# Folding the first batch's gate weights on GpSimd and ScalarE, with a fourth query buffer and a new order of TensorE's steps

## The chip, the cores and the metric

The kernel runs on one core of one Trainium2 chip. The metric is the device time of one execution in microseconds (us); the median of the runs shown stands for the kernel. A core has five engines, each of which takes its instructions in order: TensorE (PE in the profile), VectorE (DVE), ScalarE (ACT), GpSimd (POOL) and SyncE (SP), which here issues nearly all DMA transfers.

## The reference

Four batches, 12800 rows of 128 channels, 49 agents. An attention in two steps through the agents is followed by a gated convolution:

```python
a2k = sm(agents, k)              # softmax over the 12800 keys
agent_v = a2k @ v                # 49 x 128 per batch
q2a = sm(q, agents)              # softmax over the 49 agents
x = q2a @ agent_v

gate_pre = sum(conv_w[t] * shift(x, t) for t in range(5))
gate = 1 / (1 + exp(-gate_pre))
out = (gate * (x @ w_val)) @ w_out
```

All of it is float32.

## The kernel before

A batch's rows are cut into ten **units** of 1280 rows, and for the last part into 25 **chunks** of 512. Units are counted through the batches too: u10 is batch 1's first; chunks likewise, g25 is batch 1's first. The steps of the program have short names, and the list `order` gives the order in which TensorE takes them:

- `k b.u`: scores of a unit of keys (L375), 16 matmuls. ACT copies them out of PSUM (L401), DVE takes maxima (L410).
- `m b` (two steps): the maximum over all keys of a batch, as a bias for the exponentials.
- `v b.u`: exponentials on ACT (L470), a transpose of 32x32 blocks on DVE (L385), and matmuls that add up the agents' values in the bank `av` (L479).
- `f b` (five steps, `fold_weights`): agent values, convolution and weights are folded into small stationary matrices, so that the convolution runs on the agents' 49 weights and not on 128 channels. The first step normalises the agent values (`avT`, L534), multiplies them by the taps on POOL (`gw`, L539) and finds a scale (`rs`). The second does the value matmul (L562) and builds `wst`: a float16 high part and what it leaves over, for the gate (`gate_weights` L605 and `gate_rest`, through L580) and for the value (`val_weights`, L586 to L602), with copies on ACT (L620, L624). The third transposes `wst` in eight matmuls (L634) into `stat`, which DVE (L645) and ACT (L649) copy, and scales the output weight on POOL (L659). The fourth (L670) and fifth (L696) do the output weight.
- `q b.u`: scores of a unit of queries, then the softmax over agents: block transpose and row maximum on DVE (L385, L720), subtraction on POOL (L725), exponential on ACT (L733), sums and weights on DVE (L738 to L747, buffer `qw`), and a split of the weights into float16 parts in the buffer `pt`: L754 on ACT, L759 and L769 on POOL.
- `t b.u`: transposes a unit's `pt` into rows of `x`. For the first four units TensorE does it (L824), with copies by ACT (L831) and DVE (L836); for all others a DMA transpose that SP issues (L810). Then SP issues two copies of rows of x, shifted by a row for each tap, into the tile `x2` (L859), from unit 4 on once for a pair of units. POOL copies a few columns ahead of a new pair (L794).
- `g t`, `a t`, `o t`: gate (five matmuls L897 and one with the shifted rows L901), value (L924, L928) and output (L967 to L969) of a chunk. Between them stand ACT's tanh `th` (L910), DVE's product `h` (L937), its split on ACT (`hh`, L943) and POOL (`hl`, L948); ACT writes the result `ob` (L981) and SP sends it (L996).

Every step adds its operations to a planner (`Plan`), with a cost in microseconds for each and the names of the buffers that it reads and writes. TensorE keeps the order of the list. On every other engine, and for the DMAs on SP, the planner simulates its costs and takes among what is ready the operation with the longest tail of work behind it; the order that comes out is the program's. Loads of k, q and v go through a ring of eleven buffers (L368) and are issued as buffers come free.

`qw` and `pt` are rings of three, used by the unit's number:

```python
qw = ring(3, [P, NBLK, A], F32, "qw")
pts = ring(3, [P, NBLK, P], F16, "pt")
```

PSUM has two banks `sc` that all score steps and the transposes on TensorE use in turn, so a score step waits until the bank of the step before the last has been read.

Of the kernel before, what the change touches and what calls it, by code (L numbers as in the profile page):

```python
# [9 lines left out]
F32 = mybir.dt.float32  # L10
F16 = mybir.dt.float16
# [6 lines left out]
P = 128  # L18
# [5 lines left out]
NBLK = 10  # L24
# [13 lines left out]

NLOAD = 11
NT_, NH = 3, 3  # L40
NX = 4
CUT = 2
NOB = 4
# [23 lines left out]
class Plan:  # L67
# [11 lines left out]
    def add(self, engine, us, fn, reads=(), writes=(), moved=0.0, key=None, urge=0.0):  # L79
        i = len(self.steps)  # L80
        need = set()
        for x in reads:
            need |= self.wrote.get(x, set())
        for x in writes:
            need |= self.wrote.get(x, set()) | self.read.get(x, set())
        for x in reads:
            self.read.setdefault(x, set()).add(i)
        for x in writes:
            self.wrote[x], self.read[x] = {i}, set()
        self.steps.append((engine, us, fn, need, moved, key))  # L90
        self.urge.append(urge)
# [84 lines left out]
def tile_agent_attention_gated_conv(  # L176
# [25 lines left out]
    def ring(n, shape, dtype, name, pool=const):  # L202
        return [pool.tile(shape, dtype, name=f"{name}{i}") for i in range(n)]
# [9 lines left out]
    ets = ring(3, [P, NBLK, AP_], F32, "eT")  # L213
    sts = ring(2, [P, NBLK, AP_], F32, "sT")
    qmx = ring(2, [P, NBLK], F32, "qmx")
    qw = ring(3, [P, NBLK, A], F32, "qw")
    qsm = ring(2, [P, NBLK], F32, "qsm")
    qr = ring(2, [P, NBLK], F32, "qr")
    pts = ring(3, [P, NBLK, P], F16, "pt")
    x1s = ring(NX, [P, PAD + SEG], F16, "x1_")  # L220
    x2s = ring(3, [P, SEG], F16, "x2")
    ths = ring(NT_, [P, CH], F32, "th")
# [280 lines left out]
    avT = const.tile([P, A], F32, name="avT")  # L503
    mx = const.tile([P, 2], F32, name="mx")
    gw = const.tile([P, TAPS, A], F32, name="gw")
    rs = const.tile([P, 2], F32, name="rs")
    wo = const.tile([P, C], F32, name="wo")
    ro = const.tile([P, 1], F32, name="ro")
# [2 lines left out]
    def fold_weights(b):  # L511
# [92 lines left out]
        def gate_weights():  # L604
            dve.tensor_scalar_mul(ghi, gw, rs[:, 0:1])  # L605

        def gate_rest():
            gw3, hi3 = threes(gw), threes(ghi)
            twos = wst[:, 0:TAPS, 2 * A :].rearrange("p k (i r) -> p k i r", r=2)
            for r in range(2):  # L610
                rest(twos[:, :, :, r], gw3[:, :, :, r], 0, hi3[:, :, :, r])
            rest(x2g[:, :, 0:THREES], gw3[:, :, :, 2], 0, hi3[:, :, :, 2])
            rest(x2g[:, :, THREES:], gw[:, :, 3 * THREES :], 0, ghi[:, :, 3 * THREES :])

        w_ = ("wst", x)
        add("dve", 0.4, gate_weights, ["gw", "rsg"], [(*w_, "g")])
        add("dve", 1.2, val_weights, [at_v], [(*w_, "v"), "mxv"])
        add(
            "act", 0.4,
# [4 lines left out]
            "act", 0.22, lambda: nc.scalar.copy(out=wst[:, TAPS, A : 2 * A], in_=vhi),  # L624
            [(*w_, "v")], [(*w_, "e")],
        )
        add("dve", 0.7, gate_rest, ["gw", (*w_, "g")], [(*w_, "r")])
        yield
        pw_, at_w = small(b)
        pw = pw_.bitcast(F16)[:, 0 : (TAPS + 3) * P]  # L630
# [77 lines left out]
    def queries(b, u):  # L708
        g = b * NU + u
        x = g % 2  # L710
        i = slot_of["q", b, u]
        ps, at = bank()
        sT, d, e, w, r, sm = sts[x], qw[g % 3], qw[g % 3], qw[g % 3], qr[x], qsm[x]
        pt = pts[g % 3]
        sa = sT[:, :, 0:A]
        add("pe", 1.07, lambda: score_matmuls(b, ld[i], ps), [("ld", i), ("ld2", i)], [at], key="sc")
        add("dve", 0.84, lambda: transpose_blocks(sT, ps[:, :, 0:GT]), [at], [("sT", x)])
        add(
            "dve", 0.62,
            lambda: nc.vector.tensor_reduce(out=qmx[x], in_=sa, axis=AX.X, op=ALU.max),  # L720
            [("sT", x)], [("qmx", x)],
        )
        add(
            "pool", 1.05,
            lambda: nc.gpsimd.tensor_tensor(  # L725
                out=d, in0=sa, in1=qmx[x].unsqueeze(2).to_broadcast([P, NBLK, A]),
                op=ALU.subtract,
            ),
            [("sT", x), ("qmx", x)], [("qw", g % 3)],
        )  # L730
        add(
            "act", 0.6,
            lambda: nc.scalar.activation(out=e, in_=d, func=AF.Exp, scale=SCALE),  # L733
            [("qw", g % 3)], [("qw", g % 3)],
        )

        def sums():
            nc.vector.tensor_reduce(out=sm, in_=e, axis=AX.X, op=ALU.add)  # L738
            nc.vector.scalar_tensor_tensor(
                out=sm, in0=sm, scalar=1.0 / QS, in1=tiny, op0=ALU.mult, op1=ALU.add  # L740
            )
            nc.vector.reciprocal(out=r, in_=sm)

        add("dve", 0.95, sums, [("qw", g % 3)], [("qr", x)])
        add(
            "dve", 0.68,
            lambda: nc.vector.tensor_tensor(  # L747
                out=w, in0=e, in1=r.unsqueeze(2).to_broadcast([P, NBLK, A]), op=ALU.mult
            ),
            [("qw", g % 3), ("qr", x)], [("qw", g % 3)],  # L750
        )
        p_ = ("pt", g % 3)
        add(
            "act", 0.58, lambda: nc.scalar.copy(out=pt[:, :, A : 2 * A], in_=w),  # L754
            [("qw", g % 3)], [(*p_, 0)],
        )
        add(
            "pool", 0.44,
            lambda: nc.gpsimd.tensor_scalar(  # L759
                out=pt[:, :, 2 * A :].rearrange("p n (i r) -> p n i r", r=2),  # L760
                in0=w[:, :, 0 : 3 * THREES].rearrange("p n (i r) -> p n i r", r=3)[:, :, :, 0:2],
                scalar1=1.0, scalar2=0.0,
                op0=ALU.mult, op1=ALU.add,
            ),
            [("qw", g % 3)], [(*p_, 2)],
        )
        add(
            "pool", 1.09,
            lambda: nc.gpsimd.tensor_tensor(  # L769
                out=pt[:, :, 0:A], in0=w, in1=pt[:, :, A : 2 * A], op=ALU.subtract  # L770
            ),
            [("qw", g % 3), (*p_, 0)], [(*p_, 1)],
        )
    def on_pe(b, u):
        g = b * NU + u
# [25 lines left out]

    def transposes(b, u):
        g = b * NU + u
        pt = pts[g % 3]
        p_ = ("pt", g % 3)
        if not on_pe(b, u):
            dst = unit_rows(g)
            add(
# [17 lines left out]
                    identity=ident16,  # L826
                )

        add("pe", 0.65, matmuls, [("pt", g % 3, n) for n in range(3)], [at], key="t")
        add(  # L830
            "act", 0.65, lambda: nc.scalar.copy(out=dst[:, 0], in_=ps[:, 0, 0 : HB * P]),  # L831
            [at], [("x1", g // 2 % NX, g % 2)],
# [220 lines left out]
    for t in range(len(chunks) + 2):  # L1053
# [8 lines left out]
    kinds = {"m": "max", "f": "fold"}  # L1062
    order = (
# [25 lines left out]
    )  # L1089
    first = [(kinds.get(x[0], x[0]), *map(int, x[1:].split("."))) for x in order.split()]  # L1090
    for w in first:
# [70 lines left out]
```

## Time and profile before

| | |
|---|---|
| three runs | 432.86, 429.33, 430.62 us |
| median | 430.62 us |
| profiled execution | 431.12 us, its span 429.1 us |
| granted TensorE clock, mean | 0.988 |
| busy PE, DVE, ACT, POOL | 403.5, 296.1, 300.5, 226.5 us |
| DMA moved | 127.62 MB |

The span runs from the first to the last instruction. A row of the timeline has start, duration, engine, line, operation, output<-inputs and, in brackets, how long the engine had been idle and what ended that. Durations of matmuls contain a pipeline's depth, so that of back-to-back matmuls the starts are read, not the durations. A row of the windows has busy us (and instructions) of PE, PEld (weight loads), DVE, ACT and POOL, then the granted clock, the DMA engines' busy share and GB/s.

### The profile page before, as it was taken

What the parts mean: (1) busy time and instruction counts of PE and PEld (TensorE: products, weight loads), DVE (VectorE), ACT (ScalarE), POOL (GpSimd) and SP (SyncE); (2) the same over time, 40 slices, a digit from 0 to 9 for tenths busy, and PEclk for the clock granted to TensorE, in tenths of its full rate; (3) what the DMA queues carried; (4) which work ended last, traced back from release to release, by engine and by line L of the source; (5) the groups of instructions that cost most, each with busy time, mean ns of one, the idle gap of its engine ahead of it and who ended that gap; (6) DMA issues with size and microseconds to landing.
All of it is one profiled execution on the core that took longest, in us unless ns stands there. A gap on an engine that the chain in (4) does not pass through costs nothing.

```text
span 429.1 us, 10055 instructions
## 1 busy us (share of the span) xinstructions
PE 403.5 (94%) x3907; PEld 196.1 (46%) x3907; DVE 296.1 (69%) x567; ACT 300.5 (70%) x520; POOL 226.5 (53%) x258
## 2 busy tenths in 40 slices
PE   4879899999989999999999899999998899999995
PEld 2367244346545443445555343345554444434442
DVE  4666889867866978666785876667685588566231
ACT  2474468788856677778866576778984377787875
POOL 1002347664756565555467372764475466777543
PEclk9989899999999999999999999999999899999999
DMA  8999999999999999999999999999999987454833
GB/s 321 420 415 413 374 368 367 280 292 290 409 299 258 341 302 310 339 297 346 276 410 317 333 295 269 287 329 295 332 400 292 313 200 195 133 158 158 206 133 122
DMA packets 75129, 127.62 MB, mean 297 GB/s; under 512 B 50466, under 2 KB 50850, under 8 KB 75084
## 3 DMA queue, kind: packets, MB, share of 16 engines
q1 hardware_dynamic: 74940, 126.87, 95.4%
q8 instruction: 30, 0.49, 0.5%
q10 hardware_dynamic: 144, 0.13, 0.2%
q14 instruction: 15, 0.12, 0.1%
HBM read 79.25 MB, written 26.21 MB: 246 GB/s over the span
## 4 chain that ended last, share of the span: by engine, by line
PE 70%; DMA 18%; DVE 5%; issue 3%; ACT 1%; POOL 1%; SPq 1%; DVEq 0%; ACTq 0%; POOLq 0%
PE gate L897 21%; PE sc L375 16%; DMA x<-pt 8%; PE av L479 6%; PE val L924 4%; PE gate L901 4%; PE out L967 4%; DMA ld<-kT 4%; PE val L928 4%; PE out L969 4%; PE out L968 4%; DMA x<-x 3%; DMA ld<-vP 3%; POOL hl L948 1%; DVE wst L580 1%
## 5 line engine op out<-in xcount | busy, mean ns | idle before, releaser
L948 POOL TENSOR_TENSOR hl<-h,hh 128x512 f16<-128x512 f32 (+1 forms) x101 | 116.7, 1157 | 88.6 <-ACT hh L943 88.1
L897 PE MATMUL gate<-x,stat 128*128 128x512 f16 (+1 forms) x500 | 124.3, 378 | 1.6 <-ACT th L910 1.6
L937 DVE SCALAR_TENSOR_TENSOR h<-th,val 128x512 f32<-128x512 f32 x100 | 67.7, 677 | 71.1 <-PE out L968 35.7
L375 PE MATMUL sc<-ld,ag_sb 128*32 128x320 f32 x1280 | 102.1, 447 | 7.5 <-DMA ld<-kT 7.5
L910 ACT ACTIVATE th<-gate,unscale 128x512 f32<-128x512 f32 x100 | 68.3, 683 | 30.4 <-PE gate L901 28.4
L981 ACT ACTIVATE ob<-out,oscale 128x512 f32<-128x512 f32 x98 | 67.2, 686 | 19.8 <-PE out L969 18.7
L897 PEld LDWEIGHTS <-stat 128*128 128x128 f16 x505 | 45.8, 97 | 65.4 <-issue 16.6
L943 ACT CAST hh<-h 128x512 f16<-128x512 f32 (+1 forms) x101 | 61.5, 609 | 11.0 <-DVE h L937 10.5
L725 POOL TENSOR_TENSOR qw<-sT,qmx 128x490 f32<-128x490 f32 x40 | 41.5, 1039 | 44.1 <-DVE qmx L720 44.0
L375 PEld LDWEIGHTS sc<-ld,ag_sb 128*32 128x32 f32 x1280 | 36.3, 111 | 59.0 <-issue 27.6
L479 PE MATMUL av<-ld,eT 128*32 128x129 f32 (+1 forms) x1400 | 49.6, 276 | 1.5 <-DVE eT L385 1.2
L479 PEld LDWEIGHTS av<-ld,eT 128*32 128x32 f32 (+1 forms) x1400 | 46.1, 115 | 7.7 <-DVE eT L385 2.0
L401 ACT COPY ks<-sc 128x640 f32<-128x640 f32 x40 | 27.7, 692 | 28.0 <-PE sc L375 26.1
L769 POOL TENSOR_TENSOR pt<-qw,pt 128x490 f16<-128x490 f32 x40 | 45.2, 1132 | 2.5 <-ACT pt L754 2.0
L470 ACT ACTIVATE e<-ks,kbias 128x320 f32<-128x320 f32 x80 | 39.4, 553 | 4.4 <-DVE eT L385 2.9
L901 PE MATMUL gate<-x,stat 95*128 95x512 f16 x100 | 38.2, 382 | 3.2 <-DMA x<-x 3.2
L385 DVE STREAM_TRANSPOSE sT<-sc 128x640 f32<-128x640 f32 x40 | 33.5, 837 | 10.4 <-PE sc L375 10.1
L385 DVE STREAM_TRANSPOSE eT<-e 128x640 f32<-128x640 f32 x40 | 33.2, 835 | 10.4 <-ACT e L470 7.2
L967 PE MATMUL out<-hh,wo 128*128 128x512 f16 x98 | 37.5, 382 | 1.8 <-ACT ob L981 1.8
L410 DVE TENSOR_REDUCE kmx<-ks 128x2 f32<-128x640 f32 x39 | 31.5, 812 | 11.0 <-ACT ks L401 11.0
L924 PE MATMUL val<-x,stat 128*128 128x512 f16 x100 | 38.2, 382 | 0.3 <-DVE h L937 0.3
L928 PE MATMUL val<-x,stat 95*128 95x512 f16 x100 | 38.1, 381 | 0.0
(127 smaller groups left out, 397.7 us busy)
## 6 DMA issues: line engine op xcount, KB each, us to landing
ld<-kT SPq DMA_DIRECT2D x40, 640.0 KB
ld<-qT SPq DMA_DIRECT2D x40, 640.0 KB
ld<-vP SPq DMA_DIRECT2D x39, 645.0 KB
outT<-ob SPq DMA_DIRECT2D x48, 512.0 KB
x<-x SPq DMA_DIRECT2D x18, 375.0 KB
x<-x SPq DMA_DIRECT2D x18, 100.0 KB
outT<-ob SPq DMA_DIRECT2D x3, 256.0 KB
x<-x SPq DMA_DIRECT2D x4, 187.5 KB
```

Of the source, the lines that this page charges most:

```text
L375: nc.tensor.matmul(out=out[g * BLK : (g + 1) * BLK, j, 0:GT], lhsT=ag_sb[:, b, j * BLK : (j + 1) * BLK], rhs=src[:, g * GT : (g + 1) * GT] ...
L385: nc.vector.transpose(out=out.rearrange("p n (j i) -> p j n i", j=2), in_=in_.rearrange("p j (n i) -> p j n i", i=BLK),)
L479: nc.tensor.matmul(out=av[o + j : o + j + cols, 0 : C + 1], lhsT=et[:, n, j : j + cols], rhs=vt[:, n, :], start=(u == 0 and n < 2), stop=( ...
L897: nc.tensor.matmul(out=pg, lhsT=stat[:, k, :], rhs=x1[:, c : c + w], start=(k == 0), stop=False,)
L901: nc.tensor.matmul(out=pg, lhsT=stat[0 : TAPS * X2R, TAPS + 1, :], rhs=x2[0 : TAPS * X2R, o2 : o2 + w], start=False, stop=True,)
L910: lambda: nc.scalar.activation(out=th, in_=pg, func=AF.Tanh, scale=unscale[:, 0:1]),
L924: nc.tensor.matmul(out=pv, lhsT=stat[:, TAPS, :], rhs=x1s[(b * NCH + n0 // CH) // 5 % NX][:, PAD + o2 : PAD + o2 + w], start=True, stop=False,
L928: nc.tensor.matmul(out=pv, lhsT=stat[0 : TAPS * X2R, TAPS + 2, :], rhs=x2[0 : TAPS * X2R, o2 : o2 + w], start=False, stop=True,)
L937: lambda: nc.vector.scalar_tensor_tensor(out=h, in0=th, scalar=1.0, in1=pv, op0=ALU.add, op1=ALU.mult),
L943: "act", 0.16 + 0.42 * scale, lambda: nc.scalar.copy(out=hh, in_=h),
L948: lambda: nc.gpsimd.tensor_tensor(out=hl, in0=h, in1=hh, op=ALU.subtract),
L981: lambda: nc.scalar.activation(out=ob[:, o : o + w], in_=po, func=AF.Copy, scale=oscale),
```

## The change

In the first batch the gate weights leave DVE. POOL scales them into a new float32 tile `gs`, ACT rounds that into the float16 high part, and POOL subtracts in four instructions what is left over. DVE keeps the value weights. The other batches stay as they were. The rings `qw` and `pt` get four buffers. The list for TensorE is written anew: many steps change places with their neighbours. The diff, with the first, a middle and the later lines of the list:

```diff
+NPT = 4
-    qw = ring(3, [P, NBLK, A], F32, "qw")
+    qw = ring(NPT, [P, NBLK, A], F32, "qw")
-    pts = ring(3, [P, NBLK, P], F16, "pt")
+    pts = ring(NPT, [P, NBLK, P], F16, "pt")
+    gs = const.tile([P, TAPS, A], F32, name="gs")
...
+        def gate_scaled():
+            nc.gpsimd.tensor_scalar(
+                out=gs, in0=gw, scalar1=rs[:, 0:1], scalar2=1.0, op0=ALU.mult, op1=ALU.mult
+            )
+
+        def gate_rest_pool():
+            def less(out, full, hi):
+                nc.gpsimd.tensor_tensor(out=out, in0=full, in1=hi, op=ALU.subtract)
+
+            gs3, hi3 = threes(gs), threes(ghi)
+            twos = wst[:, 0:TAPS, 2 * A :].rearrange("p k (i r) -> p k i r", r=2)
+            for r in range(2):
+                less(twos[:, :, :, r], gs3[:, :, :, r], hi3[:, :, :, r])
+            less(x2g[:, :, 0:THREES], gs3[:, :, :, 2], hi3[:, :, :, 2])
+            less(x2g[:, :, THREES:], gs[:, :, 3 * THREES :], ghi[:, :, 3 * THREES :])
...
-        add("dve", 0.4, gate_weights, ["gw", "rsg"], [(*w_, "g")])
+        if b == 0:
+            add("pool", 0.4, gate_scaled, ["gw", "rsg"], ["gs"])
+            add("act", 0.4, lambda: nc.scalar.copy(out=ghi, in_=gs), ["gs"], [(*w_, "g")])
+            add("pool", 1.0, gate_rest_pool, ["gs", (*w_, "g")], [(*w_, "r")])
+        else:
+            add("dve", 0.4, gate_weights, ["gw", "rsg"], [(*w_, "g")])
...
-        add("dve", 0.7, gate_rest, ["gw", (*w_, "g")], [(*w_, "r")])
+        if b:
+            add("dve", 0.7, gate_rest, ["gw", (*w_, "g")], [(*w_, "r")])
...
     (in queries and transposes: g % 3 becomes g % NPT for qw and pt)
...
-        "v0.5 v0.6 v0.7 v0.8 v0.9 f0 t0.0 q0.1 f0 f0 k1.0 f0 k1.1 q0.2 g0 k1.2 f0 t0.1 a0 q0.3 "
-        "k1.3 q0.4 k1.4 g1 t0.2 q0.5 a1 g2 k1.5 o0 a2 t0.3 t0.4 g3 a3 o1 q0.6 g4 o2 a4 t0.5 "
+        "v0.5 v0.6 v0.7 v0.8 v0.9 f0 t0.0 f0 q0.1 k1.0 f0 k1.1 f0 q0.2 g0 k1.2 f0 t0.1 a0 q0.3 "
+        "k1.3 k1.4 q0.4 g1 t0.2 q0.5 a1 g2 k1.5 o0 a2 t0.3 t0.4 g3 a3 o1 q0.6 g4 o2 a4 t0.5 "
...
-        "v2.6 v2.7 g42 a42 o40 t2.1 g43 a43 o41 g44 a44 o42 t2.2 q2.3 v2.8 v2.9 g45 a45 o43 f2 "
-        "q2.4 f2 k3.0 g46 a46 o44 k3.1 g47 a47 o45 t2.3 f2 g48 a48 o46 f2 g49 a49 o47 f2 t2.4 "
+        "v2.6 v2.7 g42 a42 o40 t2.1 g43 a43 o41 g44 o42 a44 t2.2 q2.3 v2.8 v2.9 o43 g45 a45 f2 "
+        "g46 a46 o44 f2 q2.4 k3.0 g47 a47 o45 g48 f2 t2.3 k3.1 a48 o46 f2 g49 a49 o47 t2.4 "
...
-        "g66 o64 a66 q3.2 v3.6 v3.7 g67 a67 o65 t3.1 g68 a68 o66 g69 a69 o67 t3.2 q3.3 v3.8 "
-        "v3.9 g70 a70 o68 f3 g71 a71 o69 f3 q3.4 g72 o70 a72 f3 t3.3 g73 a73 f3 o71 g74 f3 "
+        "g66 a66 o64 q3.2 v3.6 v3.7 g67 a67 o65 t3.1 g68 a68 o66 g69 v3.8 v3.9 a69 g70 t3.2 "
+        "o67 q3.3 a70 o68 f3 g71 a71 o69 f3 q3.4 g72 o70 a72 t3.3 g73 a73 f3 o71 g74 f3 a74 "
...
```

More of the change, by code (lines that the diff above doesn't have):

```diff
@@ L712, in queries @@
         ps, at = bank()
-        sT, d, e, w, r, sm = sts[x], qw[g % 3], qw[g % 3], qw[g % 3], qr[x], qsm[x]
-        pt = pts[g % 3]
+        sT, d, e, w, r, sm = sts[x], qw[g % NPT], qw[g % NPT], qw[g % NPT], qr[x], qsm[x]
+        pt = pts[g % NPT]
         sa = sT[:, :, 0:A]
@@ L728, in queries @@
             ),
-            [("sT", x), ("qmx", x)], [("qw", g % 3)],
+            [("sT", x), ("qmx", x)], [("qw", g % NPT)],
         )
@@ L733, in queries @@
             lambda: nc.scalar.activation(out=e, in_=d, func=AF.Exp, scale=SCALE),
-            [("qw", g % 3)], [("qw", g % 3)],
+            [("qw", g % NPT)], [("qw", g % NPT)],
         )
@@ L742, in sums @@
             nc.vector.reciprocal(out=r, in_=sm)
-        add("dve", 0.95, sums, [("qw", g % 3)], [("qr", x)])
+        add("dve", 0.95, sums, [("qw", g % NPT)], [("qr", x)])
         add(
@@ L749, in queries @@
             ),
-            [("qw", g % 3), ("qr", x)], [("qw", g % 3)],
+            [("qw", g % NPT), ("qr", x)], [("qw", g % NPT)],
         )
-        p_ = ("pt", g % 3)
+        p_ = ("pt", g % NPT)
         add(
             "act", 0.58, lambda: nc.scalar.copy(out=pt[:, :, A : 2 * A], in_=w),
-            [("qw", g % 3)], [(*p_, 0)],
+            [("qw", g % NPT)], [(*p_, 0)],
         )
@@ L764, in queries @@
             ),
-            [("qw", g % 3)], [(*p_, 2)],
+            [("qw", g % NPT)], [(*p_, 2)],
         )
@@ L771, in queries @@
             ),
-            [("qw", g % 3), (*p_, 0)], [(*p_, 1)],
+            [("qw", g % NPT), (*p_, 0)], [(*p_, 1)],
         )
@@ L803, in transposes @@
         g = b * NU + u
-        pt = pts[g % 3]
-        p_ = ("pt", g % 3)
+        pt = pts[g % NPT]
+        p_ = ("pt", g % NPT)
         if not on_pe(b, u):
@@ L827, in matmuls @@
                 )
-        add("pe", 0.65, matmuls, [("pt", g % 3, n) for n in range(3)], [at], key="t")
+        add("pe", 0.65, matmuls, [("pt", g % NPT, n) for n in range(3)], [at], key="t")
         add(
```

34 rows, old and new, of the table order are left out of this document.

## The prediction

> **What bounds the kernel now.** I read the page's parts 1 and 2 first, then who waited for whom, then the timeline around each place where TensorE (PE) waits.
>
> ```profile
> PE 403.5 (94%) x3907; PEld 196.1 (46%) x3907; DVE 296.1 (69%) x567; ACT 300.5 (70%) x520; POOL 226.5 (53%) x258
> ```
>
> PE is busy 403.5 of the span's 429.1 us. Who it waited for (us in total, times, longest):
>
> ```profile
> PE sc L375 <- DMA ld<-kT: 7.5, 7, 5.8
> PE gate L901 <- DMA x<-x: 3.2, 2, 2.0
> ```
>
> The 7.5 us are for the first keys, before anything that the change touches. What else is longer than a microsecond lies, along the timeline, in four places: the fold of the first batch (L634), two waits for shifted rows x<-x (L901), and two where ScalarE (ACT) came late; their rows stand below. The rest I regard as bound by PE's own work, which the change leaves equal: the same matmuls in another order.
>
> The fold, in order of time:
>
> ```profile
> 41.20 1.28 PE L375 MATMUL sc<-ld,ag_sb 128*32 128x320 f32 x16
> ...
> 41.49 0.21 DVE L534 TENSOR_TENSOR avT<-out,den 128x49 f32<-128x49 f32 x1
> ...
> 41.78 0.60 POOL L539 TENSOR_TENSOR gw<-avT,moe_sb 128x245 f32<-128x245 f32 x1 [2.16 <-DVE avT L534]
> ...
> 42.41 0.42 PE L562 MATMUL val<-avT,moe_sb 128*128 128x49 f32 x2
> ...
> 42.50 0.47 DVE L605 TENSOR_SCALAR wst<-gw,rs 128x245 f16<-128x245 f32 x1
> ...
> 42.88 0.48 DVE L836 COPY x<-sc 128x640 f16<-128x640 f16 x1
> 43.01 0.40 ACT L620 COPY wst<-wst 128x245 f16<-128x245 f16 x1 [1.01 <-DVE wst L605]
> ...
> 43.28 0.94 DVE L580 SCALAR_TENSOR_TENSOR wst<-gw,rs,wst 128x75 f16<-128x75 f32 x4
> ...
> 43.96 0.44 PE L634 MATMUL gate<-ident,wst 128*128 128x128 f16 x5 [1.12 <-DVE wst L580]
> ...
> 44.09 0.20 DVE L586 TENSOR_REDUCE mx<-val 128x1 f32<-128x49 f32 x1
> ...
> 45.02 0.53 DVE L580 SCALAR_TENSOR_TENSOR wst<-val,rs,wst 128x30 f16<-128x30 f32 x3
> ...
> 45.42 0.42 PE L634 MATMUL gate<-ident,wst 128*128 128x128 f16 x3 [1.02 <-DVE wst L580]
> ...
> 45.46 0.84 DVE L385 STREAM_TRANSPOSE sT<-sc 128x640 f32<-128x640 f32 x1
> ...
> 45.77 1.79 PE L375 MATMUL sc<-ld,ag_sb 128*32 128x320 f32 x16
> ...
> 47.90 3.28 PE L375 MATMUL sc<-ld,ag_sb 128*32 128x320 f32 x32
> ...
> 51.11 1.25 PE L897 MATMUL gate<-x,stat 128*128 128x512 f16 x5
> ...
> 51.90 1.09 POOL L769 TENSOR_TENSOR pt<-qw,pt 128x490 f16<-128x490 f32 x1 [0.19 <-ACT pt L754]
> ...
> 53.85 0.72 PE L824 MATMUL sc<-ident,pt 128*128 128x128 f16 x10
> ```
>
> VectorE (DVE) does gate weights, gate rests and value weights one behind the other, and PE waits 1.12 and 1.02 us for them. A pass of 16 score matmuls takes 1.21 us from its start to the next (41.20 to 42.41), but the one at 45.77 takes 1.72 to the L670 transpose that follows, and two passes from 47.90 take 3.21 instead of 2.42. In 40 to 50 us the granted clock is 0.83:
>
> ```profile
> 40.00:50.00 10.00, 7.80 (x77) 3.75 (x81) 8.01 (x29) 3.11 (x6) 1.99 (x3) 0.83 1.01 366
> ...
> 60.00:70.00 10.00, 10.00 (x85) 4.52 (x82) 9.35 (x19) 8.59 (x15) 8.14 (x10) 1.00 1.02 344
> ```
>
> So the fold costs more than its waits: the slower matmuls add 0.51 + 0.79 us.
>
> **The change part by part.**
>
> *The first fold.* Off DVE come L605, 0.47, and four rests, 0.94: 1.41 us. The new chain begins at about 42.4, where gw stands (L539 ends at 42.38): a GpSimd (POOL) scaling of 245 elements, an ACT cast, four POOL subtractions (three of 75 elements, one of 20). Nothing like them stands here, but their neighbours do:
>
> ```profile
> L759 POOL TENSOR_SCALAR pt<-qw 128x300 f16<-128x300 f32 x40 | 17.9, 447 | 28.5 <-DVE qw L747 21.4 <-DMA x<-pt 7.0
> ```
>
> For the scaling I take 0.45, the row nearest in size (it could be 0.60 as L539). A POOL TENSOR_TENSOR takes 0.60 for 245 elements and 1.09 for 490, so 2.0 ns an element and 0.11 fixed: 0.26 for 75, 0.15 for 20, 0.93 for the four. The cast costs 0.40 as L620, and delays ACT's own copy L620 to 43.7, which is still early. With 0.05 at each of three hand-overs the chain ends near 42.4 + 0.45 + 0.40 + 0.93 + 0.15 = 44.3. Meanwhile DVE does the x copy and the value weights, which took 1.46 us (44.09 to 45.55), from 42.43: done at 43.9, or 44.4 with the x copy (L836, 0.48) first.
>
> PE's order there is new too: the value matmul L562 stands ahead of q0.1, so PE waits from 41.20 to 41.75 for avT (ready 41.70), then 0.42, q0.1 1.21, k1.0 1.21: 44.6, and the eight transposes find all weights ready. Both old waits, 2.14 us, become one of 0.5. PE then needs q0.1's bank, whose DVE transpose (0.84) starts at 44.4 rather than 45.46, so k1.1 runs 45.3 to 46.5, then L670 and q0.2, and g0 starts near 47.9: 3.2 us earlier. But the next step that needs a chain is t0.1. It stood 2.74 us behind g0 (51.11 to 53.85), and its operand ended 7.53 us after q0.1's DVE transpose began (45.46 to 52.99). That gives 44.4 + 7.53 = 51.9 instead of 53.85: 1.9 us. And DVE is busy 9.35 of 10 us at 60 to 70, so what lasts is about DVE's own 1.41. I take **1.5 us**, between -0.5 (POOL at half that pace, as L747 below shows for DVE: weights 1.4 us later, near 45.7, past the old 45.42) and 3.2.
>
> By the Trainium skill (SBUF — State Buffer, section "SBUF: two separate sides") a VectorE instruction with two SBUF inputs and a GpSimd instruction lock each other out for their whole length. By that, each meeting of a moved POOL instruction with such a DVE instruction would cost up to 0.85 us, and one of them on the path would leave 0.7 of the 1.5. The trace bears the rule out where such pairs meet:
>
> ```profile
> 211.28 1.15 POOL L948 TENSOR_TENSOR hl<-h,hh 128x512 f16<-128x512 f32 x1 [1.23 <-ACT hh L943]
> ...
> 211.45 1.51 DVE L747 TENSOR_TENSOR qw<-qw,qr 128x490 f32<-128x490 f32 x1
> ...
> 345.07 0.65 DVE L747 TENSOR_TENSOR qw<-qw,qr 128x490 f32<-128x490 f32 x1
> ```
>
> L747 takes 0.65 alone and 1.51 beside L948. In the first fold DVE's work reads one operand from PSUM, so I charge nothing.
>
> *Four buffers.* With three, unit u's write of pt waits until unit u-3's DMA transpose has read it. That stops ACT, which runs in order, twice:
>
> ```profile
> 127.39 0.60 ACT L754 CAST pt<-qw 128x490 f16<-128x490 f32 x1 [3.72 <-DMA x<-pt]
> ...
> 128.63 1.24 PE L897 MATMUL gate<-x,stat 128*128 128x512 f16 x5 [1.36 <-ACT th L910]
> ...
> 328.50 0.60 ACT L754 CAST pt<-qw 128x490 f16<-128x490 f32 x1 [2.63 <-DMA x<-pt]
> ...
> 329.74 0.38 PE L967 MATMUL out<-hh,wo 128*128 128x512 f16 x1 [1.83 <-ACT ob L981]
> ```
>
> Queued behind the blocked cast are th and ob, for which PE waits. With four, the write waits for u-4, whose transpose SP, also in order, issued one earlier. So 1.36 and 1.83 us go. The first counts whole: **1.36**. What is late next after the second is shown here:
>
> ```profile
> 237.13 0.39 PE L901 MATMUL gate<-x,stat 95*128 95x512 f16 x1 [1.19 <-DMA x<-x]
> ...
> 311.51 0.59 ACT L754 CAST pt<-qw 128x490 f16<-128x490 f32 x1
> ...
> 315.15 8.08 SPq L810 DMA_TRANSPOSE x<-pt  x1
> ...
> 324.43 4.06 SPq L810 DMA_TRANSPOSE x<-pt  x1
> ...
> 332.61 1.66 SPq L859 DMA_DIRECT2D x<-x  x2
> ...
> 340.01 0.59 PE L901 MATMUL gate<-x,stat 95*128 95x512 f16 x1 [2.02 <-DMA x<-x]
> 340.39 0.63 PE L924 MATMUL val<-x,stat 128*128 128x512 f16 x1
> ...
> 342.52 0.53 PE L520 MATMUL av<-fold,av 128*128 128x64 f32 x2
> ```
>
> L520 is the first f3, so the L901 before it belongs to g70, and the one at 237.13, likewise ahead of f2, to g45. Both chunks begin at a batch's unit 8 and need the shifted copy of units 8 and 9. For g70 these are u28 and u29 (counted through the batches): ACT's cast of u28 runs at 311.51, SyncE (SP) stands 8.08 us with its transpose, u29's follows at 324.43, the shifted copy at 332.61, and PE waits for it until 340.01. There the matmuls also take 0.63 rather than 0.38 us for a while. If that copy doesn't come earlier, PE only waits longer here, and the 1.83 is given back; if it comes earlier by as much, all stays. I count half: **0.92**, ends 0 and 1.83.
>
> *The order.* Mostly steps change places by one or two, with equal sums. Two moves touch the waits for x<-x. Ahead of g45 (237.13) now stands o43, three matmuls of 0.22, 0.65 us of work under the 1.19 wait: **0.65** gained. Ahead of g70 no longer stand q3.3 (1.21) and o67 (0.65): 1.86 us of cover gone, so PE comes to the same wait earlier and does that work later. If the copy stays where it is, the loss is 1.86; if it comes that much earlier, nothing. Half: **0.93** lost. The other moves I set at nothing, hidden by PE's continuous work; they could add or take one wait of the size seen, 1 to 2 us either way.
>
> Sum: 1.5 + 1.36 + 0.92 + 0.65 - 0.93 = 3.5 us. The profiled execution took 431.12, 2.0 more than its span and 0.5 above the median of 430.62 (429.33 to 432.86). 431.12 - 3.5 - 0.5 gives **427.1**, 0.8% faster than the median.
>
> **The rivals.**
>
> *The shifted copies come in time* (chance 0.27). Transposes freed from the third buffer are issued earlier, and g45 and g70 find their rows. Then 1.36 + 1.83 + 1.19 + 2.02 go, and the slow matmuls behind g70 (eight of about 0.2 extra, 1.7); with the fold 9.6 us: 421.0, or 422.2 if the copy at g45 stays late. For it: four buffers are on that path. Against: the row of u28's cast names no wait for a buffer; ACT did it late in its own order, and SP stood 8.08 us with one issue.
>
> *DMA sets the pace* (0.15). DMA's busy share is over 1 in every window I quote. If the copies at g45 and g70 land at the same absolute time, all that is won ahead is waited for there, and 1.86 us of work moved behind g70 has to follow: 431.1 - 0.5 = 430.6 without the latter, up to 432.5 with it. Against: the waits on loads are those 7.5 us, at the start.
>
> *Slower: one more transpose ahead of u29's* (0.08). If SP's order puts one more such issue ahead of the copy for g70, it comes 8.08 us later and, with the 1.86 us moved, PE loses 9.9 against the 1.5 + 1.36 + 0.65 won before: 430.6 + 6.4 = 437.0. It decides from a delay of about 6 us, since the median plus 1% is 434.9. Against: PE's order of q2.8, q2.9 against their chunks is unchanged.
>
> **How the numbers follow.** The forecast has 0.50, its own range 424.5 to 429.5 by the halves taken (0.92 and 0.93 each way, the fold from 0 to 3.2). The rivals have 0.27, 0.15 and 0.08. The range takes in the first two: 421 to 432.5, leaving about 2 in 10 beyond (the slower case, the ends of the fold). About 1% is what a measurement of this kernel can tell from no change: 426.3 and 434.9 us. Below lie the first rival and a quarter of the forecast: 0.27 + 0.13 = 0.40. Above lies 0.07. Within: 0.53.
>
> **What would show it.** Right: no ACT wait L754 <- DMA x<-pt; L634's two waits gone; clock 1.00 or near it in 40 to 50; t0.1 near 52 and g0 near 48; a wait of 2 us or more at g70. Wrong: waits at g70 gone (faster), or a growing one at g20, g45 or g70 that takes back what the fold gave; a POOL chain past 45 us; L747 or L948 lengthened beside the new POOL steps.

## The result, and the profile after

The changed kernel takes 427.03 us (median of 22 runs, 425.26 to 430.41) against 430.88 (22 runs, 427.70 to 435.20) on the same chip: a ratio of 0.9926 with a 95% interval of 0.9901 to 0.995. Ratios, here and below, compare runs in turn and leave out executions that were clearly slower than the others of their kernel, so that they differ by up to 0.003 from the quotient of the medians beside them. The forecast of 427.1 is met. How it comes about is another matter, and most of what follows is about that.

The profiled execution took 425.66 us, its span is 423.6. First the changed kernel's busy times, then whom TensorE (PE) waited for (us in total, times, longest):

```profile
PE 403.9 (95%) x3907; PEld 197.0 (47%) x3907; DVE 293.3 (69%) x562; ACT 301.5 (71%) x521; POOL 228.2 (54%) x263
```

```profile
PE sc L376 <- DMA ld<-kT: 7.0, 4, 6.1
PE gate L926 <- DMA x<-x: 1.5, 1, 1.5
PE val L432 <- DVE m L425: 1.3, 1, 1.3
PE out L994 <- POOL hl L973: 1.1, 1, 1.1
```

PE's work is the same (403.9 against 403.5 us). Its idle time falls from 429.1 - 403.5 = 25.6 us to 423.6 - 403.9 = 19.7. The two fold waits and the two waits for a late ScalarE (ACT) are no longer in the list, and of the two waits for shifted rows one is left.

The first fold, from the changed kernel's timeline (start, length, engine, line; in brackets the idle time before it and its releaser). Lines have moved: L610, L637 and L616 are the new POOL, ACT and POOL steps, L659 the former L634, L922/L926 the former L897/L901, L849 the former L824.

```profile
42.12 0.21 DVE L536 TENSOR_TENSOR avT<-out,den 128x49 f32<-128x49 f32 x1
...
43.20 0.48 POOL L610 TENSOR_SCALAR gs<-gw,rs 128x245 f32<-128x245 f32 x1 [0.19 <-DVE rs L556]
...
43.71 0.41 ACT L637 CAST wst<-gs 128x245 f16<-128x245 f32 x1 [0.74 <-POOL gs L610]
...
44.19 1.29 POOL L616 TENSOR_TENSOR wst<-gs,wst 128x75 f16<-128x75 f32 x4 [0.52 <-ACT wst L637]
...
44.33 0.53 DVE L582 SCALAR_TENSOR_TENSOR wst<-val,rs,wst 128x30 f16<-128x30 f32 x3
...
45.03 0.79 PE L659 MATMUL gate<-ident,wst 128*128 128x128 f16 x8
...
48.44 1.25 PE L922 MATMUL gate<-x,stat 128*128 128x512 f16 x5
...
52.07 0.61 PE L849 MATMUL sc<-ident,pt 128*128 128x128 f16 x8 [0.52 <-DVE sT L386]
```

Here avT came 0.63 us later than before (42.12 against 41.49), and still PE goes through its eight transposes without a wait and starts g0 at 48.44 instead of 51.11. In 40 to 50 us PE is busy 9.30 us instead of 7.80 and the clock (the column after the five engines) is 1.00 instead of 0.83:

```profile
40.00:50.00 10.00, 9.30 (x104) 4.31 (x100) 7.88 (x25) 4.43 (x10) 5.02 (x10) 1.00 1.01 364
```

Then the places where PE waited before: g18 (formerly 1.36 us behind ACT), g45, and g70 with the SyncE (SP) transfers that feed it, the transposes of u28 and u29 and their shifted copy:

```profile
126.31 1.24 PE L922 MATMUL gate<-x,stat 128*128 128x512 f16 x5
...
235.67 0.39 PE L926 MATMUL gate<-x,stat 95*128 95x512 f16 x1 [1.50 <-DMA x<-x]
...
301.94 1.84 SPq L835 DMA_TRANSPOSE x<-pt  x1
...
310.32 2.37 SPq L835 DMA_TRANSPOSE x<-pt  x1
...
323.15 1.67 SPq L884 DMA_DIRECT2D x<-x  x2
...
333.03 0.38 PE L926 MATMUL gate<-x,stat 95*128 95x512 f16 x1
```

The two transposes are issued at 301.94 and 310.32 instead of 315.15 and 324.43, the copy at 323.15 instead of 332.61, and g70's shifted matmul, at 333.03 instead of 340.01, has its rows without a wait. Of these 7.0 us 1.86 are work that now stands behind it. At g45, 1.46 us earlier than before, 0.65 us of work (o43) has been done in addition. What PE has won against the kernel before is thus 2.7 us at g0 (L922), 2.1 at g45 and about 5.1 at g70. The last is close to the whole difference of the spans, 5.5 us. From this alone one would say that g70 earned it. The experiments say that this is too simple.

### The profile page after: what moved, and what is told of

Its sections match the earlier page's. It is cut to its first block, busy times and chain, and to the rows that moved or that the text cites. A ratio compares the mean times of both kernels' runs of the same rounds, so it can differ in the third digit from the quotient of the medians.

```text
span 423.6 us, 10042 instructions
## 1 busy us (share of the span) xinstructions
PE 403.9 (95%) x3907; PEld 197.0 (47%) x3907; DVE 293.3 (69%) x562; ACT 301.5 (71%) x521; POOL 228.2 (54%) x263
## 4 chain that ended last, share of the span: by engine, by line
PE 78%; DMA 9%; DVE 8%; ACT 1%; POOL 1%; issue 1%; SPq 0%; POOLq 0%; DVEq 0%; ACTq 0%
PE gate L922 23%; PE sc L376 17%; PE av L480 10%; PE val L949 5%; PE out L992 5%; PE val L953 5%; PE gate L926 5%; PE out L993 4%; DMA ld<-kT 4%; PE out L994 4%; DMA x<-pt 3%; DMA x<-x 2%; DVE h L962 1%; DVE qw L772 1%; DVE qsm L763 1%
## 5 line engine op out<-in xcount | busy, mean ns | idle before, releaser
L922 PE MATMUL gate<-x,stat 128*128 128x512 f16 (+1 forms) x500 | 125.2, 380 | 0.2 <-ACT th L935 0.2
L922 PEld LDWEIGHTS <-stat 128*128 128x128 f16 x505 | 46.3, 97 | 63.7 <-issue 14.8
L968 ACT CAST hh<-h 128x512 f16<-128x512 f32 (+1 forms) x101 | 61.5, 609 | 17.2 <-DVE h L962 16.4
L480 PE MATMUL av<-ld,eT 128*32 128x129 f32 (+1 forms) x1400 | 50.7, 279 | 1.0 <-DVE eT L386 1.0
L480 PEld LDWEIGHTS av<-ld,eT 128*32 128x32 f32 (+1 forms) x1400 | 47.1, 117 | 7.5 <-issue 2.5
L926 PE MATMUL gate<-x,stat 95*128 95x512 f16 x100 | 38.3, 383 | 1.5 <-DMA x<-x 1.5
L994 PE MATMUL out<-hl,wo 128*128 128x512 f16 x98 | 37.0, 378 | 1.1 <-POOL hl L973 1.1
```

What stands on the lines that cost most here:

```text
L480: nc.tensor.matmul(out=av[o + j : o + j + cols, 0 : C + 1], lhsT=et[:, n, j : j + cols], rhs=vt[:, n, :], start=(u == 0 and n < 2), stop=( ...
L922: nc.tensor.matmul(out=pg, lhsT=stat[:, k, :], rhs=x1[:, c : c + w], start=(k == 0), stop=False,)
L926: nc.tensor.matmul(out=pg, lhsT=stat[0 : TAPS * X2R, TAPS + 1, :], rhs=x2[0 : TAPS * X2R, o2 : o2 + w], start=False, stop=True,)
L968: "act", 0.16 + 0.42 * scale, lambda: nc.scalar.copy(out=hh, in_=h),
```

## The experiments

All ratios are to the kernel before, run in turn with them on the same chip, over five rounds; brackets hold 95% intervals. The first four kernels shared one chip (the kernel before 430.41, 23 runs). The theories were: the fold earns it, the buffers earn it, or the order of PE's list earns it.

**Four buffers alone.**

```diff
-    qw = ring(3, ...)    pts = ring(3, ...)    g % 3
+    qw = ring(NPT, ...)  pts = ring(NPT, ...)  g % NPT      (NPT = 4)
```

> The kernel before with four buffers for qw and pt and nothing else; on every engine the instructions stand in the order of before, so only the waits on the buffers differ. Theory A (the recorded prediction): ACT's waits at 127 and 328 us go, the first 1.36 us stays won, of the second 1.83 about half is given back at g70, which still waits for its shifted rows: 1.4 to 3.2 us less, ratio 0.993 to 0.997, g70's wait 2 us or longer. Theory B (the buffers bring the transposes of u28 and u29 forward, and that is what emptied the wait at g70 in the changed kernel): 6 us less, ratio 0.986, u28's transpose issued near 302 us, no wait at g70. Theory C (the DMA queue sets the pace): nothing, ratio 0.999 to 1.001, the waits for x<-x grow by what ACT's waits were.

Measured: 430.63 us, 0.9996 [0.9966, 1.0025]. No engine's instruction order differs from the kernel before, so this is the effect of two waits taken away and nothing else. ACT waits for no transpose any more, and PE's 1.36 us at g18 are gone. The timeline of this kernel at g70 (its L811 is the transpose, L902 the former L901):

```profile
313.71 7.72 SPq L811 DMA_TRANSPOSE x<-pt  x1
...
322.94 3.92 SPq L811 DMA_TRANSPOSE x<-pt  x1
...
338.28 0.38 PE L902 MATMUL gate<-x,stat 95*128 95x512 f16 x1 [4.17 <-DMA x<-x]
```

SP stands 7.72 us with u28's transpose as before (8.08), the rows land 1.7 us earlier than before, and PE, which now comes earlier, waits 4.17 us instead of 2.02. The buffers move the waiting from ACT to g70. This one execution keeps a lead of 1.7 us behind g70; the ratio over all runs shows none.

**The order alone.**

```diff
-        "v0.5 v0.6 v0.7 ... "          (the whole list of before)
+        "v0.5 v0.6 v0.7 ... "          (the whole list of the change; three buffers, old fold)
```

> The kernel before with the new order of TensorE's steps, and what the planner makes of it on the other engines; three buffers, gate weights on DVE. ACT's cast of u28 stands behind 60 tanh instructions instead of 65. Theory A (order a wash, 0.65 won at g45, 0.93 lost at g70): within 1 us of before, ratio 0.998 to 1.002, g70 still waits. Theory D (the order alone brings u28's transpose forward, and empties g70's wait and the slow matmuls behind it): 3 to 5 us less, ratio 0.989 to 0.993, u28's transpose issued 10 us or more earlier than 315 us; the wait of ACT at 127 us stays. Theory C: nothing.

Measured: 427.80 us (6 runs), 0.9919 [0.989, 0.9949]: by the ratio the whole gain of the change, by the medians 2.6 of its 3.9 us. Its timeline:

```profile
47.37 0.61 PE L634 MATMUL gate<-ident,wst 128*128 128x128 f16 x8 [2.69 <-DVE wst L580]
...
303.51 2.57 SPq L810 DMA_TRANSPOSE x<-pt  x1
...
312.64 2.34 SPq L810 DMA_TRANSPOSE x<-pt  x1
...
335.39 0.38 PE L901 MATMUL gate<-x,stat 95*128 95x512 f16 x1
```

The new list makes the old fold worse (one wait of 2.69 us instead of 2.14 in two), and the kernel gains none the less. u28 and u29 are transposed 12 us earlier and g70 doesn't wait, with three buffers and without the new fold. ACT's stops behind a DMA transpose shrink too, from 6.4 us in two to 1.0 us in one, without a fourth buffer, and g18 doesn't wait.

**The fold alone.**

```diff
+        if b == 0: (gate_scaled on POOL, cast on ACT, gate_rest_pool on POOL)
+        else:      (gate_weights and gate_rest on DVE, as before)
```

> The kernel before with the first batch's gate weights on GpSimd and ScalarE alone; old order, three buffers. Theory A: the second wait of the eight weight transposes (1.02 us) shrinks by 0.5 to 1 us, g0 starts 0.5 to 1.5 us earlier; 0.3 to 1 us less, ratio 0.998 to 0.9995. Rival: the value matmul still stands behind q0.1 in this order, so DVE ends the value weights no earlier than 44.3 us and POOL is not the gain: under 0.3 us, ratio 0.9995 to 1.001.

Measured: 430.67 us, 1.0006 [0.9981, 1.003]. In its timeline:

```profile
44.57 0.85 PE L659 MATMUL gate<-ident,wst 128*128 128x128 f16 x8 [1.44 <-POOL wst L616]
...
49.11 1.25 PE L922 MATMUL gate<-x,stat 128*128 128x512 f16 x5
...
96.13 0.39 PE L926 MATMUL gate<-x,stat 95*128 95x512 f16 x1 [2.69 <-DMA x<-x]
```

With PE's old steps the POOL chain is waited for, 1.44 us. g0 still starts 2.0 us earlier (49.11 against 51.11), and at 96.13 (g10) PE waits 2.69 us for shifted rows, where it waited for none before.

**The change with three buffers.**

```diff
-NPT = 4
+NPT = 3
```

> The changed kernel with three buffers instead of four; every engine's instructions in the order of the changed kernel, so only the waits on the buffers differ. Theory A and D: ACT's wait near 125 us comes back (1 to 1.5 us of PE), the one at 328 does not, since u28's transpose is issued near 302: 1 to 1.5 us more than the changed kernel, ratio to before 0.994 to 0.997. Theory B: g70 waits again, 4 to 6 us more than the changed kernel, ratio to before 0.999 or above.

Measured: 426.83 us (6 runs), 0.9897 [0.9866, 0.9928]. The fourth buffer isn't needed for the gain. ACT's stop near 125 us, which was expected back, doesn't come; ACT stops once elsewhere, and PE with it, ahead of g43:

```profile
226.92 0.60 ACT L779 CAST pt<-qw 128x490 f16<-128x490 f32 x1 [4.84 <-DMA x<-pt]
```

```profile
228.16 1.03 PE L922 MATMUL gate<-x,stat 128*128 128x512 f16 x4 [3.04 <-ACT th L935]
```

These 3.04 us replace the wait for shifted rows at g45, which this kernel doesn't have. The parts multiply to 0.9996 x 0.9919 x 1.0006 = 0.9921, against 0.9926 measured. The three intervals leave some 0.5% either way for this product, about 2 us, so that it shows nothing left for the three to do together, and doesn't exclude a microsecond or two.

The next theory was that the order earns by bringing the transposes for g70 forward. Four kernels tried it (another chip, the kernel before 431.07, 29 runs).

**One step moved**, the second m3 behind g59 and a59:

```diff
-        "t2.7 m3 g58 a58 o56 m3 g59 a59 o57 ..."
+        "t2.7 m3 g58 a58 o56 g59 a59 m3 o57 ..."
```

> The kernel before with one step of the list moved: the second m3 behind g59 and a59 instead of ahead of them. Three buffers, gate weights on DVE. In the program that comes out, ACT's cast of u28 stands behind 60 tanh instructions instead of 65, and its transpose on SP behind 29 result transfers instead of 32; u29's stay where they were. Theory D1 (u28's transpose, issued late and holding SP for 8.08 us, is what makes g70 wait): transpose of u28 issued 8 us or more earlier, g70's wait of 2.0 us and the slow matmuls behind it gone, ACT's wait at 328 too; 2.5 to 4 us less, ratio 0.991 to 0.994. Rival D2 (u29's, which isn't moved, is the one that g70 waits for, and it is late by itself): the wait at g70 stays at 1.5 to 2.5 us, ratio 0.998 to 1.002.

Measured: 433.82 us, 1.0074 [1.0037, 1.011]. u28's transpose is issued at 306.48 and g70 waits no more; but this is in its timeline, first GpSimd (POOL), then PE:

```profile
303.46 0.19 POOL L794 COPY x<-x 128x4 f16<-128x4 f16 x1 [9.64 <-DMA x<-pt]
```

```profile
304.81 0.59 PE L969 MATMUL out<-hl,wo 128*128 128x512 f16 x1 [3.64 <-POOL hl L948]
```

POOL's small copy, issued in order, stands 9.64 us waiting for a transpose to land; hl is queued behind it, and PE waits 3.64 us for hl.

**The late part of the order alone.** The two lists differ in 46 groups of neighbouring steps; this kernel takes 13 of them, from k3.1 to g70.

```diff
-        "... k3.1 g47 a47 o45 ... g69 a69 o67 t3.2 q3.3 v3.8 v3.9 g70 ..."
+        "... g47 a47 o45 g48 f2 t2.3 k3.1 ... g69 v3.8 v3.9 a69 g70 t3.2 o67 q3.3 ..."
```

> The kernel before with the new order between a46's neighbourhood (k3.1) and g70 only, 13 groups of moves out of 46, the second m3 and the cover of g70 (q3.3 and o67 behind it) among them. Theory D: this is the stage where the new order earns, so most of order_only's 0.9919 is here: ratio 0.990 to 0.994, no wait at g70, waits at 127 and 237 us as before. Rival (the gain is spread over many small moves): 0.996 to 0.999.

Measured: 432.66 us, 1.0042 [1.0002, 1.0082]. There is no wait for shifted rows left in its profile at all, not even at g45, ahead of all of PE's steps that were moved, and it isn't faster. Why it is slower isn't shown.

**Transposes urged in the planner**, in the kernel before and in the changed one:

```diff
-            [(*p_, n) for n in range(3)], [("x1", g // 2 % NX, g % 2)], 2.4,
+            [(*p_, n) for n in range(3)], [("x1", g // 2 % NX, g % 2)], 2.4, urge=8.0,
```

> The kernel before, its own order, three buffers; the planner's tail of each DMA transpose is 8 us longer, so that what leads to it is done earlier on ACT, POOL, DVE and SP. ACT's cast of u28 stands behind 62 tanh instructions instead of 65, that of u29 behind 63; both transposes behind 31 result transfers instead of 32. Theory D (late transposes cost the time, whatever brings them forward): g70's wait shrinks to under 1 us; 1.5 to 4 us less, ratio 0.991 to 0.9965. Rival (the DMA queue's length sets the landing, not the time of issue): g70's wait stays near 2 us, ratio 0.998 to 1.003.

> The changed kernel with the same 8 us on the tail of each DMA transpose. ACT's casts of u18 and u19 stand behind 37 and 38 tanh instructions instead of 40 and 40. Theory D: the one long wait for shifted rows that is left, 1.5 us at g45 with slow matmuls behind it, goes: 1.5 to 3 us less than the changed kernel, ratio to before 0.985 to 0.989. Rival (work that is pulled forward delays th, ob and the folds by as much): the same as the changed kernel or slower, ratio to before 0.991 to 0.997.

Measured: 436.27 us, 1.0144 [1.01, 1.0189], and 434.37 us, 1.009 [1.0052, 1.0128]. Urging costs 1.4% in the kernel before, and the changed kernel, 0.9926 without it, comes to 1.009. The waits of the first, of the second, and the second's timeline:

```profile
POOL x L794 <- DMA x<-pt: 30.8, 6, 9.9
```

```profile
POOL x L819 <- DMA x<-pt: 38.9, 9, 7.1
```

```profile
346.56 0.58 PE L994 MATMUL out<-hl,wo 128*128 128x512 f16 x1 [2.31 <-POOL hl L973]
```

POOL waits 30.8 us for transposes in the first, against 24.9 in the kernel before, and 38.9 in the second, against 16.4 and 22.6 in two executions of the changed kernel. PE waits for POOL's hl (2.96 us in the first, at 268.97, and 2.31 here) and for ACT's `ob` (2.39 and 2.60). So the theory fell: none of the four kernels has a wait of PE for shifted rows at g70, and none is faster than before. That wait can disappear while PE waits elsewhere.

The last theory was that the early part of the list earns it (a third chip, the kernel before 430.83, 35 runs).

**The early part alone**: the first 20 of the 46 groups, to g46.

```diff
-        "... f0 t0.0 q0.1 f0 f0 k1.0 f0 k1.1 ... g44 a44 o42 t2.2 q2.3 v2.8 v2.9 g45 a45 o43 f2 ..."
+        "... f0 t0.0 f0 q0.1 k1.0 f0 k1.1 f0 ... g44 o42 a44 t2.2 q2.3 v2.8 v2.9 o43 g45 a45 f2 ..."
```

> The kernel before with the first 20 of the 46 groups of moves: the new order up to g46, the old one behind it. Three buffers, gate weights on DVE. ACT's casts and SP's transposes of u28 and u29 stand where they stood before, so g70 keeps its wait. Theory E (the order earns ahead of g46, at 127 us and g45, and the late part gives nothing or takes a little, as late_part measured): 2 to 4 us less, ratio 0.990 to 0.995, g70 still waits 2 us or more. Rival (the parts work only together, since each shifts when the other's transfers land): ratio 0.997 to 1.004.

Measured: 429.16 us, 0.9978 [0.9945, 1.0011]: a quarter of the order's gain, and not distinguishable from none. Its timeline, first at g43, then at g70:

```profile
228.14 1.77 PE L897 MATMUL gate<-x,stat 128*128 128x512 f16 x4 [2.68 <-ACT th L910]
...
315.11 5.11 SPq L810 DMA_TRANSPOSE x<-pt  x1
...
336.96 0.39 PE L901 MATMUL gate<-x,stat 95*128 95x512 f16 x1
```

g70 was expected to keep its wait of 2 us or more, and in this execution it has none, although u28's transpose is issued when it was before (315.11 against 315.15): SP stands 5.11 us with it instead of 8.08. So the move of that transpose in SP's queue isn't the only way to an empty wait at g70.

**The fold with its own steps of the list**, groups 0 to 2 (the value matmul ahead of q0.1), three buffers.

```diff
-        "v0.5 v0.6 v0.7 v0.8 v0.9 f0 t0.0 q0.1 f0 f0 k1.0 f0 k1.1 q0.2 g0 ..."
+        "v0.5 v0.6 v0.7 v0.8 v0.9 f0 t0.0 f0 q0.1 k1.0 f0 k1.1 f0 q0.2 g0 ..."   (with the new fold)
```

> The kernel before with the gate weights on GpSimd and ScalarE and the three moves of the list inside the first fold (value matmul ahead of q0.1, the third step behind k1.0, the fourth behind k1.1); three buffers, everything else in the old order. The recorded prediction: 1.5 us less, between 0.5 more and 3.2 less, ratio 0.9965, g0 2 to 3 us earlier and t0.1 1.9 us earlier. Rival, after fold_only (g0 was 2.0 us earlier there, and a wait for shifted rows at g11 took it back): g0 earlier as forecast, but a new wait of 1 us or more for shifted rows before 130 us, ratio 0.999 to 1.001.

Measured: 430.09 us, 1.0004 [0.9968, 1.004]. The fold has its order now and no wait at L659, and the gain is gone all the same:

```profile
96.06 0.39 PE L926 MATMUL gate<-x,stat 95*128 95x512 f16 x1 [3.07 <-DMA x<-x]
...
339.72 0.38 PE L926 MATMUL gate<-x,stat 95*128 95x512 f16 x1 [2.02 <-DMA x<-x]
```

**The change with the 13 late groups in the old order, and the change again.**

```diff
-        "... g47 a47 o45 g48 f2 t2.3 k3.1 ... g70 t3.2 o67 q3.3 ..."     (of the change)
+        "... k3.1 g47 a47 o45 ... t3.2 q3.3 v3.8 v3.9 g70 ..."           (of before)
```

> The changed kernel with the list's 13 groups between k3.1 and g70 put back into the old order. Theory E: the late part costs 0.4% by late_part, so this is 1 to 2 us faster than the changed kernel, ratio to before 0.985 to 0.990, with g70's wait of 2 us or more back and the losses between 285 and 307 us gone. Rival (in the changed kernel the late part earns, by the empty wait at g70): 2 to 4 us slower than the changed kernel, ratio 0.996 to 1.001.

> The changed kernel again, unaltered, on the chip of the three kernels above, for a comparison on the same chip. By its first measurement: ratio 0.990 to 0.995 to before. Its profile shows which of its waits (1.5 us at g45, none at g70, none of ACT on a DMA) come back from one execution to the next: by theory A to E all of them; if the landing of transfers varies between executions, waits for shifted rows change by 1 us or more.

Measured: 428.84 us, 0.9965 [0.9918, 1.0013] without the late part; 426.36 us, 0.9927 [0.9889, 0.9964] for the change itself, as on the first chip. By these values the late groups are worth some 0.4% inside the changed kernel, where alone they cost 0.4%; but the two intervals overlap, and five of the twelve runs without the late part took 425.0 to 427.1 us, as the changed kernel does, the others 428.7 to 431.7. In the traced one, of 430.44 us, g70's old wait is back, and a longer one stands at g10:

```profile
97.20 0.58 PE L926 MATMUL gate<-x,stat 95*128 95x512 f16 x1 [3.25 <-DMA x<-x]
...
339.08 0.59 PE L926 MATMUL gate<-x,stat 95*128 95x512 f16 x1 [2.28 <-DMA x<-x]
```

The second can't come from the late part: up to 217 us every engine has the same instructions in the same order as in the changed kernel, which at g10 waits for nothing in one of its two executions and 0.33 us in the other. Those two differ as well. The second has a wait for shifted rows at g0 that the first hadn't, and at g45 1.32 us instead of 1.50; g70 is empty in both:

```profile
50.46 0.38 PE L926 MATMUL gate<-x,stat 95*128 95x512 f16 x1 [1.12 <-DMA x<-x]
```

A wait for shifted rows can thus come and go by 1 to 3 us between executions of the same instructions, and one trace doesn't show that an edit made it.

**What stays open.** That the order alone earns the gain, or most of it, is shown. Which of its groups do isn't. The early part's 0.9978 and the late part's 1.0042 multiply to 1.002, and the whole list gives 0.9919: either the 13 groups behind g70, which were not tried by themselves, hold the rest, or early and late groups only pay together. The kernel with new early and tail groups, fold and buffers (0.9965) speaks against much lying in the tail alone, but its interval is too wide to settle it. No version tried beats the change by more than the intervals allow; three buffers in place of four do as well.

## Why the prediction was right, point by point

The number was right by luck: its largest terms were not what made it.

*The fold, -1.5: the place right, the size wrong.* Scaling (0.48 for 0.45), cast (0.41 for 0.40), g0 (48.44 for 47.9), t0.1 (52.07 for 51.9), the clock of 1.00 and the end of both L634 waits came as described. The four POOL subtractions took 1.29 us, not 0.93, and the chain ended at 45.48 (44.19 + 1.29), past the 45 that I had named as a sign against me; with avT 0.63 later it still cost nothing. No DVE row beside the new POOL work is longer than before (L582 0.53 as L580 was), so charging nothing for such meetings held; no DVE instruction with two SBUF inputs was among them, so this fold doesn't test that case. The wrong step is "what lasts is about DVE's own 1.41". In the two kernels with the fold but not the rest, a wait for shifted rows at g10 takes 2.69 and 3.07 us, and nothing lasts: 1.0006 and 1.0004. (That the fold makes this wait isn't shown, since g10 also waited 3.25 us in an execution of the changed kernel's early instructions.) The lower ends of their intervals leave at most 0.8 us (0.9981) and 1.4 us (0.9968). My range for this term contained zero; my value should have been near it.

*Four buffers, -1.36 and -0.92: mechanism right, both sizes wrong.* The ACT waits on transposes are gone. I counted the first whole and asked only of the second what is late next. In the trace the answer is the same for both: g70's rows. By the measured ratio the two terms, 2.28 us in the sum, are 0.2 us together, and the interval reaches from 1.5 us won to 1.1 lost (0.9966 and 1.0025 of 430). The buffer rival fell as well: four buffers don't bring the transposes of u28 and u29 forward, for SP stands 7.72 us with u28's as it stood 8.08. What I had put against that rival was right.

*The order, +0.65 and -0.93, together 0.28 lost: wrong by sign and size.* It gives 427.80 against 430.41 by the medians, 2.6 us or 0.6%, and about 3.5 us or 0.8% by the ratio. o43 ahead of g45 didn't shorten that wait in the change (1.50 and 1.32 us in two executions, 1.19 before). Ahead of g70 I had weighed only the two steps moved past it. What I did not follow is that the list also sets the planner's order on the other engines: ACT's cast of u28 stands behind 60 of its tanh steps instead of 65, SP's transpose of it behind 29 result transfers instead of 32. With the early part of the list alone these counts stay at 65 and 32, and g70's wait is gone in its trace all the same, so they are one cause and not the whole. "A wait of 2 us or more at g70" is the step that failed outright. I had set "the other moves" at nothing, "hidden by PE's continuous work", and 1 to 2 us either way; they are the gain.

*The rivals.* "The shifted copies come in time" has the profile's g70 right, by the order and not by the buffers, but g45 still waits and the time isn't 421. "DMA sets the pace" comes near to what the fold and the buffers did when each was alone, no time won (430.67 and 430.63 us, forecast 430.6); but its landings at the same absolute time don't show: with four buffers g70's rows came at 338.28 instead of 340.01. The slower rival's mechanism, SP held longer ahead of g70, is not what the slower kernels show: their losses, as far as they are seen, are at POOL's copy and hl (m3 moved, urged transposes) and at ACT's `ob` (urged).

So the sum came out at 3.5 because 3.78 us for fold and buffers, which the runs don't show, stood in for an order of about the same worth that I had counted at -0.28. That the two agree is luck.

## What to carry to other kernels

When several in-order engines share one stream of transfers, a stall that is removed ahead of the next landing may be waited for there, as with the four buffers here: ask of each term of a sum, also the first, which landing comes next and whether the edit moves it. A hand-written order for one engine that feeds a planner is an edit to every engine's queue; compare the queues before costing it at nothing. And a wait that disappears from the profile isn't yet time won: the late part and the moved m3 both empty g70 and are slower. Nor does one trace tell an edit's wait from one that comes and goes by itself. So try the parts by themselves, and trace the same kernel twice.

## What the hardware showed that was not expected

SP stood 1.84 us with u28's DMA transpose at 301.94 in the change and 8.08 us with the same one at 315.15 before. A POOL copy of 128x4 elements, 0.19 us of work, held its engine for 9.64 us and PE behind it for 3.64. Four POOL subtractions, three of which take every third element of `gs`, took 1.29 us, where my estimate from the rows of 245 and 490 elements was 0.93. Waits of the same length don't always slow the matmuls behind them: behind 2.02 us at g70 they took 0.63 us in the kernel before (340.39) and 0.38 in the kernel with the fold and its own steps (339.93). Behind the 1.50 us at g45 in the change they took 0.63 (239.35), with a granted clock of 0.83 in 234 to 244 us; behind 1.32 us in its second execution they took 0.38, with a clock of 1.00. One profiled execution can stand over 2 us from the median of its kernel (430.34 against 432.66 for the late part), so its waits show mechanisms, and the ratios alone show gains of this size.
